# Larger q and k tiles in fewer buffers: 14, 12, 12 and 12 chunks with three buffers in place of five tiles of ten with four

## The chip, the core and the metric

The kernel runs on one core of a Trainium2 chip. The core has a matmul engine (PE, whose weight loads are listed apart as PEld), three engines for elementwise work (DVE, ACT and POOL), a queue engine (SP), and 16 DMA engines which all queues share. Each engine works through its own instructions in order; semaphores tie the engines together. The metric is the device time of one execution in microseconds. A DMA that changes the type of its data, here float32 in HBM to bfloat16 on the chip, is issued from POOL in this kernel.

## What is computed

Inputs are q, k and v of shape 4 x 6400 x 256 and the weights of a mixture of eight small adapters. For each of the four batches a 256 x 256 attention matrix is formed over the 6400 rows, applied to v, and every output row then gets the sum of its two best adapters:

```python
qn = q / (np.linalg.norm(q, axis=1, keepdims=True) + 1e-06)
kn = k / (np.linalg.norm(k, axis=1, keepdims=True) + 1e-06)
s = kn.transpose(0, 2, 1) @ qn / tau
a = softmax(s)                      # over the last axis
x = v @ a                           # 25600 rows of 256
logits = x @ w_gate                 # 8 experts, the best two kept
w = softmax over the two
out = x + sum over the two of w * ((x @ A[e]) @ B[e])
```

## The kernel before

A batch has 6400 rows, which are cut into 50 chunks of 128 rows. A chunk of q, k or v is 128 partitions by 256 elements. q and k of one chunk take 0.262 MB in HBM, v of one chunk 0.131 MB. All inputs together are 78.6 MB, the output is 26.2 MB.

**Two kinds of work.** The first is the Gram stage of a batch: for each chunk `gram` (L211) adds k transposed times q into the PSUM tile `acc` (two matmuls, L217), `square` (L199) squares two chunks of q and k, and `norm` (L222) adds up the squares by matmuls (L228 for batch 0, L234 for the others). When all 50 chunks are in, seven short functions `chain0` to `chain6` turn `acc` and the norms into the attention matrix `a_bf` and into `wa_sb`, the attention matrix times the gate and adapter weights. The second kind is the row stage: for each pair of chunks of v, `transposes` (L366) turns the rows over, `logits` and `gating` choose the experts for a group of five pairs, `z_gz` (L472, L476) multiplies by the adapters and weighs them by the gates into the tile `gz`, `gz_t` (L496 to L502) turns that over into `gzT`, `y_mm` (L488) multiplies v by the attention matrix, and `delta` (L508, L512) adds the adapters' part and copies the result to the staging tile `ys`.

**The order.** The whole order is written out by hand. Batch 0's Gram stage runs alone, at the beginning. After it come 100 slots, one for each pair of v's chunks, 25 to a batch, in one loop on all engines. In the loop the Gram stages of batches 1, 2 and 3 are spread over slots 0 to 20, 24 to 45 and 49 to 67, some two or three chunks to a slot (`todo`). A slot s transposes pair s; z, gz and y of a pair come several slots later, once its group's gates are ready. Chunk c of batch 1 falls in slot c*21//50, so that chunks 10 and 11 are in slot 4, chunk 14 in slot 5, chunk 26 in slot 10.

**Loads.** q and k of a batch come in five tiles of ten chunks (`PC = 10`), each filled by two DMAs (L148 for q, L149 for k). The first four chunks of batch 0 come on SP in float32 instead, and batch 0's last tile comes in parts of 6 and 4. v comes in tiles of 18, 16 and 16 chunks (L151), which for batch 0 are loaded in two parts each (10 and 8, 8 and 8, 8 and 8). There are four buffers for tiles of q and k and three for v. All these loads are in one list, sorted by the slot in which each is first needed. `qk_need` gives that slot for a tile of q and k; for v it is the number of the pair plus one. The sort keeps the order of the list where slots are equal, and q and k were put in first. `load_more` (L129) issues from the head of the list and stops at a tile whose buffer is still to be read by work not yet written out, so POOL issues loads in exactly this order. On POOL the issue waits for the release of the buffer, and everything behind it waits along.

Read in this order, the list before begins: batch 0's q and k; batch 1's q and k tile 0; the first part of v's first tile; q and k tile 1; the second part of v's first tile (v chunks 10 to 17); q and k tile 2; the first part of v's second tile (v chunks 18 to 25); q and k tile 3; and so on.

**Stores.** The output leaves from nine `ys` tiles of ten chunks. ACT issues the stores (L529). Up to seven finished groups are held back while loads are still to come (`DEFER`); from slot 67 on the number held back falls. The last ten pairs go out in smaller pieces on SP (L516).

**Working buffers.** `gz` and `gzT` rotate through three buffers each (`work`), and `ae`, the exponentiated attention matrix of a batch, through two (`bat`).

Of the kernel before, what the change touches and what calls it, by code (L numbers as in the profile page):

```python
# [9 lines left out]
BF16 = mybir.dt.bfloat16  # L10
# [6 lines left out]
def kernel(  # L17
# [17 lines left out]
    B, N, C = q.shape  # L35
    P = 128
    NC = N // P
    CC = C // P
# [3 lines left out]
    assert ER == P and CC == 2 and N % P == 0  # L42
    inv_tau = 1.0 / float(tau)

    PC = 10
    NPAIR = NC // 2
    NPT = B * NPAIR
    GRP = 5
    QKB, VB, YB = 4, 3, 9
    VP = [18, 16, 16]  # L50
    FIRST = 4
    DEFER = 7

# [9 lines left out]
    qk_pool = ctx.enter_context(tc.tile_pool(name="qkp", bufs=QKB))  # L63
    v_pool = ctx.enter_context(tc.tile_pool(name="vp", bufs=VB))
# [3 lines left out]
    bat = ctx.enter_context(tc.tile_pool(name="bat", bufs=2))  # L68
    one = ctx.enter_context(tc.tile_pool(name="one", bufs=1))
    gwork = ctx.enter_context(tc.tile_pool(name="gwork", bufs=3))  # L70
    work = ctx.enter_context(tc.tile_pool(name="work", bufs=3))
    ps_acc = ctx.enter_context(tc.tile_pool(name="psacc", bufs=1, space=bass.MemoryType.PSUM))
    ps_nrm = ctx.enter_context(tc.tile_pool(name="psnrm", bufs=1, space=bass.MemoryType.PSUM))
    ps_t = ctx.enter_context(tc.tile_pool(name="pst", bufs=2, space=bass.MemoryType.PSUM))
# [6 lines left out]

    todo = {}
    qk_need = {}
    for b, (first, last) in GRAM.items():
        n = last - first + 1
        for c in range(NC):
            s = first + c * n // NC
            todo.setdefault(s, []).append((b, c))
            qk_need.setdefault((b, c // PC), s)


    loads = []

    for s in range(NC // PC):
        o = FIRST if s == 0 else 0
        loads.append((-10 + s, "qk", 0, s, o, [6, 4] if s == NC // PC - 1 else [PC - o]))
        for b in range(1, B):
            loads.append((qk_need[b, s], "qk", b, s, 0, [PC]))
    for b in range(B):
        for s, n in enumerate(VP):  # L100
            at = NPAIR * b + sum(VP[:s]) // 2 + 1
            if b == 0:

                loads.append((at, "v", b, s, 0, [n - 8]))
                loads.append((at + (n - 8) // 2, "v", b, s, n - 8, [8]))
            else:
                loads.append((at, "v", b, s, 0,
                              [8, 4, 4] if b == B - 1 and s == len(VP) - 1 else [n]))
    loads.sort(key=lambda x: x[0])
    tiles = {"qk": {}, "v": {}}  # L110
    left = {"qk": [], "v": []}
    bufs = {"qk": QKB, "v": VB}
    where = {}
    at_load = [0]

    def piece(kind, c):

        if kind == "qk":
            return divmod(c, PC)
        s = 0  # L120
        while c >= VP[s]:
            c -= VP[s]
            s += 1
        return s, c

    def used(kind, b, c, n):
        left[kind][where[kind, b, piece(kind, c)[0]]] -= n

    def load_more(limit=1000):  # L129

        while limit and at_load[0] < len(loads):
            _, kind, b, s, o, parts = loads[at_load[0]]
            if (kind, b, s) not in where:
                n = len(left[kind])
                if n >= bufs[kind] and left[kind][n - bufs[kind]]:
                    return
                where[kind, b, s] = n
                left[kind].append(PC if kind == "qk" else VP[s])
                if kind == "qk":
                    t = qk_pool.tile([P, 2, PC, C], BF16, tag="qk", name="qk")  # L140
                else:
                    t = v_pool.tile([P, max(VP), C], BF16, tag="v", name="vt")
                tiles[kind][b, s] = t
            t = tiles[kind][b, s]
            c0 = s * PC if kind == "qk" else sum(VP[:s])
            for m in parts:
                if kind == "qk":
                    nc.gpsimd.dma_start(t[:, 0, o:o + m, :], q_v[b, :, c0 + o:c0 + o + m, :])  # L148
                    nc.gpsimd.dma_start(t[:, 1, o:o + m, :], k_v[b, :, c0 + o:c0 + o + m, :])  # L149
                else:  # L150
                    nc.gpsimd.dma_start(t[:, o:o + m, :], v_v[b, :, c0 + o:c0 + o + m, :])  # L151
                o += m
            at_load[0] += 1
            limit -= 1
# [11 lines left out]
    nc.sync.dma_start(bst, moe_B.rearrange("e r d -> (e r) d"))  # L166
    nc.sync.dma_start(ast, moe_A.rearrange("e (p cc) r -> p e (cc r)", p=P))
    load_more(3)
    ones_bf = const.tile([P, P], BF16)
    nc.vector.memset(ones_bf, 1.0)  # L170
# [4 lines left out]
    for c in range(0, FIRST, 2):  # L175
        t = tiles["qk"][0, 0]
        nc.vector.tensor_copy(t[:, 0, c:c + 2, :], stage[:, 0, c:c + 2, :])
        nc.scalar.copy(t[:, 1, c:c + 2, :], stage[:, 1, c:c + 2, :])
    load_more(1)
    ident = const.tile([P, P], BF16)  # L180
    make_identity(nc, ident)
    ident_f = const.tile([P, P], FP32)
    make_identity(nc, ident_f)
    load_more(3)

    wg_sb = const.tile([P, CC, E], BF16)
# [11 lines left out]

    def square(b, c, eng):  # L199

        s, o = divmod(c, PC)
        t = tiles["qk"][b, s]
        sq = sq_pool.tile([P, 2, 2, C], BF16, tag="sq", name="sq")
        sqs[b, c] = sq
        src = t[:, :, o:o + 2, :]
        if eng == "act":
            nc.scalar.activation(sq, src, ACT.Square)  # L207
        else:
            nc.vector.tensor_tensor(out=sq, in0=src, in1=src, op=OP.mult)  # L209

    def gram(b, c):  # L211
        if c == 0:
            acc[b] = ps_acc.tile([P, CC, C], FP32, tag="acc", name="acc")
        s, o = divmod(c, PC)
        t = tiles["qk"][b, s]
        for ic in range(CC):
            nc.tensor.matmul(  # L217
                acc[b][:, ic, :], t[:, 1, o, ic * P:(ic + 1) * P], t[:, 0, o, :],
                start=(c == 0 and ic == 0), stop=(c == NC - 1), skip_group_check=True)
        used("qk", b, c, 1)  # L220
# [60 lines left out]

    def chain3(b):
        d = st[b]
        ae = bat.tile([P, CC, C], BF16, name="ae")
        se = bat.tile([P, CC], FP32, name="se")
        for ic in range(CC):
            nc.scalar.activation(ae[:, ic, :], d["s"][:, ic, :], ACT.Exp, bias=neg_inv_tau[:, 0:1],
                                 scale=inv_tau, accum_out=se[:, ic:ic + 1])
        d["ae"], d["se"] = ae, se
# [37 lines left out]
    def chain6(b):  # L327
        d = st[b]
        a_bf = bat.tile([P, CC, C], BF16, name="a_bf")
        for ic in range(CC):  # L330
# [3 lines left out]


    CHAIN = [(chain0, 0.0), (chain1, 0.9), (chain2, 0.75), (chain3, 0.0), (chain4, 0.55),
             (chain5, 0.65), (chain6, 0.5)]

# [14 lines left out]
    def transposes(g, eng):  # L353

        b, p = divmod(g, NPAIR)
        gr = groups[g]
        if "vT" not in gr:
            gr["vT"] = vt_pool.tile([P, CC, 2 * GRP, P], BF16, tag="vT", name="vT")
        s, o = piece("v", 2 * p)
        vt = tiles["v"][b, s]  # L360
        full = ps_t.tile([P, 512], FP32, tag="pt", name="vT_ps")
        pt = full[:, 0:256].bitcast(BF16).rearrange("p (c t) -> p c t", c=CC)
        i = 0
        for sc in range(2):
            for ic in range(CC):
                nc.tensor.matmul(pt[:, ic, sc * P:(sc + 1) * P],  # L366
                                 vt[:, o + sc, ic * P:(ic + 1) * P], ident,
                                 is_transpose=True, start=(i == 0), stop=(i == 3))
                i += 1
        used("v", b, 2 * p, 2)  # L370
        w = 2 * (g - gr["f"])
        dst = gr["vT"][:, :, w:w + 2, :]
        src = pt.rearrange("p c (s t) -> p c s t", s=2)
        if eng == "act":
            nc.scalar.copy(dst, src)  # L375
        else:
            nc.vector.tensor_copy(dst, src)  # L377
        gr["full"] = full
        pr[g] = {"vT": dst, "w": w}
# [152 lines left out]
    for c in range(0, NC, 2):  # L532
        square(0, c, "act" if (c // 2) % 2 else "dve")
        gram(0, c)
        gram(0, c + 1)
        load_more()
        if c >= 4:
            norm(0, c - 4)
            norm(0, c - 3)
# [7 lines left out]
    def gram_part(items):  # L547
        for b, c in items:
            gram(b, c)
            if c >= 2:  # L550
                norm(b, c - 2)
            if c == NC - 1:
                norm(b, c - 1)
                norm(b, c)
# [18 lines left out]
    while nz < NPT or zq is not None or dq is not None:  # L573
# [7 lines left out]
        for b, c in items:  # L581
            if c % 2 == 0:
                square(b, c, "act")
        if f in (chain0, chain1, chain2, chain3):
            f(fb)
# [70 lines left out]
```

## Time and profile before

| | |
|---|---|
| median of three runs | 255.92 us (255.84 to 256.08) |
| the profiled execution | 255.87 us |
| its span, first to last instruction | 254.1 us |
| PE busy, share of the span | 220.4 us, 87% |
| ACT busy | 176.1 us, 69% |
| DVE busy | 152.7 us, 60% |
| POOL busy | 33.0 us, 13% |
| HBM read and written | 78.91 MB and 26.21 MB, 414 GB/s over the span |
| POOL's queue of loads | 8496 packets, 74.8% of the 16 DMA engines' time |
| ACT's queue of stores | 2592 packets, 22.4% |

Busy time of PE contains pipelined matmuls, so a busy PE is not one at its peak. GB/s in the slices and windows counts bytes as they land on the chip; a load is read from HBM at twice that, as it turns float32 into bfloat16. A DMA share can be above 1, since packets of one DMA engine overlap. "Time to landing" of an issue runs from the issue on the queue to the last byte's semaphore, with all that lies ahead of it in the DMA engines.

### The profile page before, as it was taken

Reading aid. Unit: us, or ns where it says so; the run is one execution under the profiler, and the core shown is the slowest. Engines: PE = TensorE matmul, PEld = TensorE weight load, DVE = VectorE, ACT = ScalarE, POOL = GpSimd, SP = SyncE. Lnnn points to the kernel's source line nnn. Section 1 sums busy time; section 2 is a strip of 40 time slices with the busy share of each in tenths; the row PEclk is TensorE's granted clock in tenths of the full one; section 3 lists DMA queues with packets and bytes.
Section 4 is the critical chain, followed back from the end, with each engine's and each line's share of the span. In section 5 each row is a group of like instructions: output and inputs, shape, how many; then the busy total and the mean of one; then the engine's idle time right before and its main releaser. Section 6 shows DMA issues by size and latency. Waiting matters only on the chain.

```text
span 254.1 us, 7393 instructions
## 1 busy us (share of the span) xinstructions
PE 220.4 (87%) x3106; PEld 190.2 (75%) x3106; DVE 152.7 (60%) x577; ACT 176.1 (69%) x290; POOL 33.0 (13%) x67
## 2 busy tenths in 40 slices
PE   0787793985999999999999989999999899999950
PEld 0444461775899978989999778989997799998940
DVE  1322235453567678685776876767587876778720
ACT  3434344776488698887878778888867777887860
POOL 8131221112112100110110202000000200000000
PEclk9999998696899999999999999999999999999997
DMA  7999999999999999999999999999999999999995
GB/s 213 223 217 215 212 216 214 213 216 216 210 214 215 223 207 215 218 212 214 215 220 211 214 270 259 236 296 281 255 291 292 389 326 362 414 420 426 423 412 220
DMA packets 13745, 66.80 MB, mean 263 GB/s; under 512 B 2576, under 2 KB 2704, under 8 KB 10384
## 3 DMA queue, kind: packets, MB, share of 16 engines
q0 software_dynamic: 8496, 38.80, 74.8%
q10 hardware_dynamic: 2592, 23.59, 22.4%
q1 hardware_dynamic: 2624, 3.94, 4.7%
q8 instruction: 24, 0.39, 0.6%
q14 instruction: 9, 0.07, 0.1%
HBM read 78.91 MB, written 26.21 MB: 414 GB/s over the span
## 4 chain that ended last, share of the span: by engine, by line
PE 58%; DMA 25%; DVE 7%; ACT 3%; issue 2%; POOL 1%; DVEq 0%; POOLq 0%; ACTq 0%
DMA qk<-in_k_dram 20%; PE y_ps L488 15%; PE acc L217 11%; PE zg L472 7%; PE y_ps L508 7%; PE vT_ps L366 6%; DMA out_dram<-ys 5%; PE zg L496 4%; PE nrm L234 3%; PE vT_ps L387 3%; ACT sq L207 2%; DVE gz L476 2%; ACT ys L512 1%; DVE lm L422 1%; DVE e L418 1%
## 5 line engine op out<-in xcount | busy, mean ns | idle before, releaser
L207 ACT ACTIVATE sq<-qk 128x1024 bf16<-128x1024 bf16 x87 | 89.6, 1054 | 22.1 <-DMA qk<-in_k_dram 16.8
L217 PE MATMUL acc<-qk 128*128 128x256 bf16 x400 | 74.7, 287 | 15.3 <-DMA qk<-in_k_dram 8.8
L512 ACT COPY ys<-y_ps 128x512 f32<-128x512 f32 x100 | 58.8, 588 | 22.9 <-PE y_ps L508 19.7
L488 PE MATMUL y_ps<-a_bf,vT 128*128 128x256 bf16 x400 | 60.3, 273 | 0.3 <-ACT ys L512 0.3
L217 PEld LDWEIGHTS <-qk 128*128 128x128 bf16 x400 | 34.4, 102 | 25.4 <-DMA qk<-in_k_dram 11.8
L476 DVE TENSOR_TENSOR gz<-zg,gate 128x256 bf16<-128x256 f32 x100 | 41.7, 418 | 14.7 <-PE zg L472 13.4
L377 DVE COPY vT<-vT_ps 128x512 bf16<-128x512 bf16 x63 | 26.7, 424 | 28.2 <-PE vT_ps L366 27.6
L234 PEld LDWEIGHTS <-sq 128*128 128x128 bf16 x600 | 36.3, 98 | 7.2 <-ACT sq L207 3.1
L366 PE MATMUL vT_ps<-ident,vt 128*128 128x128 bf16 x400 | 39.5, 223 | 0.9 <-DMA vt<-in_v_dram 0.7
L472 PE MATMUL zg<-wa_sb,vT 128*128 128x128 bf16 x400 | 38.7, 220 | 1.2 <-DVE gzT L502 1.0
L508 PE MATMUL y_ps<-ball_sb,gzT 128*128 128x256 bf16 x200 | 38.2, 273 | 0.0
L234 PE MATMUL nrm<-ones_bf,sq 128*128 128x1 bf16 x600 | 35.9, 165 | 1.2 <-ACT sq L207 1.2
L488 PEld LDWEIGHTS <-vT 128*128 128x128 bf16 x400 | 33.6, 97 | 3.2 <-issue 0.4
L366 PEld LDWEIGHTS <-vt 128*128 128x128 bf16 x400 | 30.2, 99 | 3.4 <-DMA vt<-in_v_dram 0.8
L496 PE MATMUL zg<-ident,gz 128*128 128x128 bf16 x200 | 27.9, 222 | 1.1 <-DVE gz L476 0.6
L375 ACT COPY vT<-vT_ps 128x512 bf16<-128x512 bf16 x37 | 21.7, 587 | 10.3 <-PE vT_ps L366 8.9
L472 PEld LDWEIGHTS <-vT 128*128 128x128 bf16 x400 | 26.1, 97 | 3.4 <-issue 2.2
L502 DVE COPY gzT<-zg 128x256 bf16<-128x256 bf16 x90 | 25.3, 281 | 0.0
L148 POOL DMA_DIRECT2D qk<-in_q_dram x21 | 11.4, 545 | 91.1 <-ACT sq L207 23.6
L209 DVE TENSOR_TENSOR sq<-qk 128x1024 bf16<-128x1024 bf16 x13 | 9.0, 693 | 22.3 <-DMA qk<-in_k_dram 15.4
L496 PEld LDWEIGHTS <-gz 128*128 128x128 bf16 x200 | 15.3, 99 | 2.9 <-DVE gz L476 2.5
L151 POOL DMA_DIRECT2D vt<-in_v_dram x17 | 9.0, 534 | 64.4 <-PE y_ps L508 45.5
(61 smaller groups left out, 183.6 us busy)
## 6 DMA issues: line engine op xcount, KB each, us to landing
out_dram<-ys ACTq DMA_DIRECT2D x18, 1280.0 KB, 13.1
qk<-in_q_dram POOLq DMA_DIRECT2D x18, 640.0 KB, 20.9
qk<-in_k_dram POOLq DMA_DIRECT2D x18, 640.0 KB, 23.1
vt<-in_v_dram POOLq DMA_DIRECT2D x5, 1024.0 KB, 26.9
vt<-in_v_dram POOLq DMA_DIRECT2D x3, 1152.0 KB, 25.3
vt<-in_v_dram POOLq DMA_DIRECT2D x6, 512.0 KB, 22.1
out_dram<-ys SPq DMA_DIRECT2D x3, 512.0 KB, 8.7
out_dram<-ys SPq DMA_DIRECT2D x4, 256.0 KB, 7.6
```

The source lines that it names most:

```text
L207: nc.scalar.activation(sq, src, ACT.Square)
L217: nc.tensor.matmul(acc[b][:, ic, :], t[:, 1, o, ic * P:(ic + 1) * P], t[:, 0, o, :], start=(c == 0 and ic == 0), stop=(c == NC - 1), skip_ ...
L234: nc.tensor.matmul(nrm[b][:, j:j + 1], sq[:, w, c % 2, ic * P:(ic + 1) * P], ones_bf[:, 0:1], start=(c == 0 and j == 0), stop=(c == NC - 1 ...
L366: nc.tensor.matmul(pt[:, ic, sc * P:(sc + 1) * P], vt[:, o + sc, ic * P:(ic + 1) * P], ident, is_transpose=True, start=(i == 0), stop=(i = ...
L377: nc.vector.tensor_copy(dst, src)
L472: nc.tensor.matmul(z[:, sc, :], r["vT"][:, ic, sc, :], st[b]["wa"][:, ic, E:E + ER], start=(sc == 0 and ic == 0), stop=(sc == 1 and ic == ...
L476: nc.vector.tensor_tensor(out=gz.rearrange("p c (e r) -> p c e r", e=E), in0=z.rearrange("p c (e r) -> p c e r", e=E), in1=gr["gate"][:, r ...
L488: nc.tensor.matmul(y[:, sc, :], r["vT"][:, ic, sc, :], st[b]["a"][:, ic, :], start=(sc == 0 and ic == 0), stop=False, skip_group_check=True)
L496: nc.tensor.matmul(gt[:, sc, :], r["gz"][:, sc, :], ident, is_transpose=True, start=(sc == 0), stop=(sc == 1))
L502: nc.vector.tensor_copy(gzT, gt)
L508: nc.tensor.matmul(r["y"][:, sc, :], r["gzT"][:, sc, :], ball_sb, start=False, stop=(sc == 1), skip_group_check=True)
L512: nc.scalar.copy(gr["ys"][:, r["w"]:r["w"] + 2, :], r["y"])
```

## The change

Tiles of q and k have 14, 12, 12 and 12 chunks in place of five times 10, and three buffers in place of four. Batch 0's last tile is loaded in parts of 8 and 4. The helper `piece`, which used to look up v's uneven tiles, now serves q and k too; the lists of sizes stand together in `PARTS`. The tile in memory always has room for 14 chunks, so three of them take 43,008 bytes of a partition where four of ten chunks took 40,960. `work` goes from three buffers to two, and `ae` from two to one, which frees 2,048 bytes between them. Nothing else differs: the order of the matmuls, squares and copies is the same.

```diff
-    PC = 10
-    QKB, VB, YB = 4, 3, 9
-    VP = [18, 16, 16]
+    QKB, VB, YB = 3, 3, 9
+    PARTS = {"qk": [14, 12, 12, 12], "v": [18, 16, 16]}
...
-    work = ctx.enter_context(tc.tile_pool(name="work", bufs=3))
+    work = ctx.enter_context(tc.tile_pool(name="work", bufs=2))
...
+    def piece(kind, c):
+        s = 0
+        while c >= PARTS[kind][s]:
+            c -= PARTS[kind][s]
+            s += 1
+        return s, c
+
...
-            qk_need.setdefault((b, c // PC), s)
+            qk_need.setdefault((b, piece("qk", c)[0]), s)
...
-    for s in range(NC // PC):
+    for s, n in enumerate(PARTS["qk"]):
         o = FIRST if s == 0 else 0
-        loads.append((-10 + s, "qk", 0, s, o, [6, 4] if s == NC // PC - 1 else [PC - o]))
+        last = s == len(PARTS["qk"]) - 1
+        loads.append((-10 + s, "qk", 0, s, o, [n - 4, 4] if last else [n - o]))
         for b in range(1, B):
-            loads.append((qk_need[b, s], "qk", b, s, 0, [PC]))
+            loads.append((qk_need[b, s], "qk", b, s, 0, [n]))
...
-                    t = qk_pool.tile([P, 2, PC, C], BF16, tag="qk", name="qk")
+                    t = qk_pool.tile([P, 2, max(PARTS[kind]), C], BF16, tag="qk", name="qk")
...
-            c0 = s * PC if kind == "qk" else sum(VP[:s])
+            c0 = sum(PARTS[kind][:s])
...
-        s, o = divmod(c, PC)
+        s, o = piece("qk", c)
...
-        ae = bat.tile([P, CC, C], BF16, name="ae")
+        ae = one.tile([P, CC, C], BF16, name="ae")
```

More of the change, by code (lines that the diff above doesn't have):

```diff
@@ L88 @@
             todo.setdefault(s, []).append((b, c))
-            qk_need.setdefault((b, c // PC), s)
+            qk_need.setdefault((b, piece("qk", c)[0]), s)
     loads = []
-    for s in range(NC // PC):
+    for s, n in enumerate(PARTS["qk"]):
         o = FIRST if s == 0 else 0
-        loads.append((-10 + s, "qk", 0, s, o, [6, 4] if s == NC // PC - 1 else [PC - o]))
+        last = s == len(PARTS["qk"]) - 1
+        loads.append((-10 + s, "qk", 0, s, o, [n - 4, 4] if last else [n - o]))
         for b in range(1, B):
-            loads.append((qk_need[b, s], "qk", b, s, 0, [PC]))
+            loads.append((qk_need[b, s], "qk", b, s, 0, [n]))
     for b in range(B):
-        for s, n in enumerate(VP):
-            at = NPAIR * b + sum(VP[:s]) // 2 + 1
+        for s, n in enumerate(PARTS["v"]):
+            at = NPAIR * b + sum(PARTS["v"][:s]) // 2 + 1
             if b == 0:
@@ L107 @@
                 loads.append((at, "v", b, s, 0,
-                              [8, 4, 4] if b == B - 1 and s == len(VP) - 1 else [n]))
+                              [8, 4, 4] if b == B - 1 and s == len(PARTS["v"]) - 1 else [n]))
     loads.sort(key=lambda x: x[0])
@@ L114 @@
     at_load = [0]
[L116 to L124, printed above, removed]
     def used(kind, b, c, n):
@@ L137, in load_more @@
                 where[kind, b, s] = n
-                left[kind].append(PC if kind == "qk" else VP[s])
+                left[kind].append(PARTS[kind][s])
                 if kind == "qk":
-                    t = qk_pool.tile([P, 2, PC, C], BF16, tag="qk", name="qk")
+                    t = qk_pool.tile([P, 2, max(PARTS[kind]), C], BF16, tag="qk", name="qk")
                 else:
-                    t = v_pool.tile([P, max(VP), C], BF16, tag="v", name="vt")
+                    t = v_pool.tile([P, max(PARTS[kind]), C], BF16, tag="v", name="vt")
                 tiles[kind][b, s] = t
             t = tiles[kind][b, s]
-            c0 = s * PC if kind == "qk" else sum(VP[:s])
+            c0 = sum(PARTS[kind][:s])
             for m in parts:
@@ L213, in gram @@
             acc[b] = ps_acc.tile([P, CC, C], FP32, tag="acc", name="acc")
-        s, o = divmod(c, PC)
+        s, o = piece("qk", c)
         t = tiles["qk"][b, s]
```

## The prediction

> **What bounds the kernel now.** I read first the slices of the page, then a table of 5 us windows. Its columns are stretch, length, busy time (x instructions) of PE, PEld, DVE, ACT and POOL, granted PE clock, share of the DMA engines' time, GB/s.
>
> ```profile
> DMA  7999999999999999999999999999999999999995
> ...
> 15.00:20.00 5.00, 3.93 (x29) 2.75 (x29) 1.39 (x2) 3.14 (x3) 1.98 (x4) 1.00 1.10 217
> 55.00:60.00 5.00, 2.35 (x43) 2.02 (x42) 3.03 (x14) 1.47 (x4) 0.53 (x1) 0.92 1.05 213
> 60.00:65.00 5.00, 5.00 (x53) 4.32 (x52) 2.10 (x6) 3.72 (x4) 1.06 (x2) 0.50 1.07 218
> 75.00:80.00 5.00, 5.00 (x95) 4.72 (x91) 3.43 (x15) 4.40 (x8) 0.87 (x2) 1.00 1.06 213
> 245.00:250.00 5.00, 0.47 (x5) 0.18 (x2) 0.00 (x0) 1.02 (x2) 0.00 (x0) 1.00 0.96 390
> ```
>
> Two limits lie close together. The DMA engines are full from 5 us to 249 us, so the bytes alone nearly fill the span. PE waits for loads up to about 62 us (3.93 and 2.35 busy of 5), and from then on is busy 4.5 to 5.0 of 5 until the last work at 246 us. So 62 to 246 us is a nearly rigid train of slots: what is late at 62 us is late at 246 us. The PE timeline shows the waits where the train starts:
>
> ```profile
> 53.64 0.40 PE L366 MATMUL vT_ps<-ident,vt 128*128 128x128 bf16 x4 [0.71 <-DMA vt<-in_v_dram]
> 56.73 0.38 PE L472 MATMUL zg<-wa_sb,vT 128*128 128x128 bf16 x4
> 59.77 0.61 PE L217 MATMUL acc<-qk 128*128 128x256 bf16 x2 [2.65 <-DMA qk<-in_k_dram]
> ...
> 62.45 0.59 PE L366 MATMUL vT_ps<-ident,vt 128*128 128x128 bf16 x4
> ```
>
> 53.64 is slot 5, which transposes chunks 10 and 11 of v; 62.45 is slot 9, chunks 18 and 19. Both pieces are in the views of single issues of line 151: issue time, then time to landing.
>
> ```profile
> L151 POOL DMA_DIRECT2D vt<-in_v_dram x1: 530/530/530, 32.6 to 32.6; - x1
> ...
> DMA to landing us min/median/max: 21.0/21.0/21.0
> ...
> L151 POOL DMA_DIRECT2D vt<-in_v_dram x1: 527/527/527, 39.1 to 39.1; - x1
> ...
> DMA to landing us min/median/max: 23.0/23.0/23.0
> ```
>
> They land at 53.6 and 62.1 us. The tail and one late wait come from the same view of the last store, and from the list of waits:
>
> ```profile
> L516 SPq DMA_DIRECT2D out_dram<-ys x1: 462/462/462, 246.1 to 246.1; - x1
> ...
> DMA to landing us min/median/max: 6.9/6.9/6.9
> ...
> ACT ys L512 <- DMA out_dram<-ys: 1.7, 1, 1.7
> ```
>
> **The change, part by part.** *Landing order.* POOL issues the loads in one sorted list, and the DMA engines work it off in that order. A chunk of q and k is 0.262 MB in HBM, a chunk of v half that. In the list before, 20 chunks of batch 1's q and k (tiles 0 and 1) stand ahead of the second piece of v's first tile, and 30 ahead of v's chunk 18. In the new list these are 14 + 12 = 26, and 14 + 12 + 12 = 38: the third tile's first use and this v piece both fall on slot 10, and the sort keeps q and k first. The read rate comes from landings: batch 0's last k (12.06 MB read) at 16.41 + 19.37 = 35.8 us, v's chunk 18 (23.33 MB) at 62.1, so 26.3 us for 11.27 MB, 2.33 us per MB. Six more chunks are 1.57 MB or 3.7 us, eight are 2.10 MB or 4.9 us. The two v pieces land at 57.3 and 67.0 us. Nothing covers this: slot 5 is already waiting at 53.64, and slot 9 cannot transpose before 67.0, 4.55 us after 62.45. Queued behind that wait is all of PE; DVE's vT copy and ACT's squares and copies follow it.
>
> *The clock.* After the 2.65 us wait PE ran at half clock (0.50 in 60:65; normal slots return at 66). Slots 9 to 12 took 62.45 to 70.16, 7.7 us with 3.5 of it at half clock, against 4 slots in 8.04 us later (68.31 to 76.35), 6.0 for three. PE will now stand some 3.5 us ahead of slot 5 and 1.5 to 4 us ahead of slot 9. If the clock stays full, three slots take 6.0 and the train is 4.55 - 1.7 = 2.9 us late; with the 6.2 us of half clock that the 59.8 wait brought (1.7/3.5 us lost per us) it is 4.55 + 1.3 = 5.9. The wait ahead of slot 9 follows a stretch that will be slow already, so I lean to the upper half: 5.0. The Trainium skill ("TensorE: Matmul & The Clock Gate", Part 1: The HAM clock gate) speaks against the change here: an idle window of about 3.4 us halves the clock, a busy one of that length restores it. By this rule alone 3.4 us would be slow after 67.0, as many as before, so 4.5 us late and an end of about 257.0.
>
> *Phase 0.* The last piece but one is 8 chunks for 6. It lands 1.05 MB (2.5 us) before 35.8, so at 33.3, and PE needs 4 pairs of 0.87 us (0.87 is the step from 16.09 to 16.97): ready for the last piece at 36.8, 1.0 us late. Slot 0 goes from 46.5 to 47.5, and its first v piece lands at 47.4 too, 4 chunks later than 45.0. Both end in the wait of slot 5: nothing more.
>
> *Fewer, larger transfers.* q and k go from 21 to 17 DMAs each. Eight issues of 0.53 us leave POOL, which is 13% busy: nothing. On the DMA engines the saving is not shown: at least 0; at most one mean packet (74.8% of 16 x 254.1 us over 8496 packets, 0.36 us) for each of 8, 2.9 us. I take 0.3, near the bottom, since stretches of 10-chunk q/k transfers and of 16 and 18-chunk v ones run alike at 213 to 216 GB/s. The Trainium skill ("DMA: Bandwidth & Descriptors", Anatomy of one DMA) gives each such DMA a fixed 2.0 us beside its bytes; eight fewer in series would be 16 us, an end near 240. The landings agree with bytes alone, since seven others are in flight.
>
> *Three buffers of q/k.* A load now waits on the tile three back. The tightest is batch 3's first: released at slot 35 (118.3 us, and some 6 later now), while the load ahead of it lands at 128.8 as before (102.30 + 26.5). The margin falls from 17.6 us (issued at 111.2) to about 4.7. The shortest landing of a POOL load is 6.3 us (the first, 0.79 MB, 1.8 us of it bytes): 4.5 us of start. It just holds: cost 0, at most 1.8 us at each of four such waits. v's loads stand behind it on POOL.
>
> *Two buffers of gz and gzT, one of ae.* DVE's gz write waits for the transposes of two slots ago, its gzT copy for the delta matmuls two before; PE is in order and has done both ahead of the matmuls that DVE waits for anyway. Cost 0. Uncovered, each of 100 slots could pay a PE group of 0.28 us. ae of the batch before was last read 20 slots earlier: 0.
>
> *The sum.* The train is 5.0 late. At 194.6 ACT waited 1.7 us for a store to free a ys buffer; stores will find the DMA engines less loaded, and this wait goes. PE lost 0.5 of 5 us in 191:196, so 0.6 comes back: 4.4. What of it shows? The last store took 6.9 us to land, behind others, where the first load (0.52 MB, empty queues) took 3.6: up to 3.3 us are hidden by the queue. On the other side the DMA share is already 0.98 in 196:199, so idle DMA time there may be added in full: 0 hidden. I take 2.5, nearer the last store's own row, as it is the one that ends the run. 4.4 - 2.5 - 0.3 = 1.6. Profiled run 255.87 us (span 254.1, 1.8 around it; median of three 255.92): **257.5 us**. Its own range: 2.9 late, 3.3 hidden, 0.3 saved, 255.5; 5.9 late, none hidden, 260.9, of which I keep 259.5.
>
> **The rivals.** *Not slower: the tail hides it all.* The DMA engines are the sole bound; bytes are equal; the lateness stays below the 3.3 us of queue. For it: the full DMA row. Against: 4.4 is above 3.3. It decides if the clock stays full at slot 9: 2.9 - 0.6 = 2.3. Time 255.87 - 0.3 = 255.6; with more saved per transfer, up to 2.9, 253.0. *Starved queue.* The 4.7 us margin is too short and loads stop at four releases, while stores are still held back. For it: half of the margin gone. Against: 15 us and more in hand today. Two to four stops of 1.8 us take the place of the hidden part: 259.5. *The two-buffer wait bites*: 100 slots of 0.28 us, 284; the program order speaks against it.
>
> **How the numbers follow.** Forecast 0.70, hidden tail 0.18, starved queue 0.10, buffers 0.02. What a measurement can tell from no change is 0.2%, 0.5 us. Of the forecast, 0.04 falls below 256.4 (same) and none lower; the hidden tail splits 0.13 faster, 0.05 same. Faster 0.13, same 0.09, slower 0.78. The range takes the forecast's own and reaches into the hidden tail: 255.3 to 259.8.
>
> **What would show it.** Right: slot 5's transposes near 57.3 and slot 9's near 67.0, each ended by a v load; half clock reaching 70 us or beyond; the last ys copy near 250; the wait of 1.7 us on ys gone; a shorter landing of the last store. Wrong: slot 9 before 64, a later v piece without a later end, or DMA slices below 9 between 110 and 170 us (then the queue starves).

## The result, and the profile after

| | before | after |
|---|---|---|
| median of five runs | 256.02 us (255.84 to 256.08) | 259.38 us (258.52 to 259.94) |
| ratio, 95% interval | | 1.013 (1.0105 to 1.0154) |
| the profiled execution | 255.87 us | 259.80 us |
| its span | 254.1 us | 258.0 us |
| HBM rate over the span | 414 GB/s | 407 GB/s |
| packets on POOL's queue, share of the DMA engines' time | 8496, 74.8% | 7344, 73.8% |
| last `ys` copy ends | 246.09 us | 251.14 us |

The change costs 3.4 us by the medians, 3.9 us between the two profiled executions. The forecast was 257.5 us: right in direction, and less than half of the loss.

The PE timeline of after, at the two waits for v (start, length, engine, line, operation, and in brackets the idle time before it with what ended it):

```profile
57.23 0.40 PE L365 MATMUL vT_ps<-ident,vt 128*128 128x128 bf16 x4 [2.30 <-DMA vt<-in_v_dram]
...
67.06 0.61 PE L365 MATMUL vT_ps<-ident,vt 128*128 128x128 bf16 x4 [3.44 <-DMA vt<-in_v_dram]
...
70.56 0.63 PE L365 MATMUL vT_ps<-ident,vt 128*128 128x128 bf16 x4
```

Slot 5 starts at 57.23 and slot 9 at 67.06, both ended by the landing of a v piece; the forecast had 57.3 and 67.0. Slot 9 now sits 4.61 us behind its old 62.45. It runs at half clock (0.61 us for four transposes where 0.40 is normal), and slot 11 starts at 73.62 us, 5.31 us late. From there the train is rigid: 5.31 at slot 62, 5.50 at slot 71, 4.95 at slot 74, 5.05 at the last `ys` copy.

Both pieces again in the views of single issues:

```profile
L150 POOL DMA_DIRECT2D vt<-in_v_dram x1: 550/550/550, 35.4 to 35.4; - x1
...
DMA to landing us min/median/max: 21.7/21.7/21.7
...
L150 POOL DMA_DIRECT2D vt<-in_v_dram x1: 558/558/558, 40.7 to 40.7; - x1
...
DMA to landing us min/median/max: 26.4/26.4/26.4
```

They are issued 2.8 and 1.6 us later than before, and the second has 3.4 us more ahead of it in the DMA engines (26.4 against 23.0).

The row of DMA slices and the windows of after, with the columns of the windows before (the last three are PE clock, DMA share, GB/s):

```profile
DMA  7999999999999999999999999999999999999994
...
55.00:60.00 5.00, 2.77 (x53) 2.46 (x54) 2.14 (x9) 1.65 (x3) 2.12 (x4) 0.89 1.06 216
60.00:65.00 5.00, 3.63 (x48) 3.18 (x46) 2.86 (x11) 4.23 (x6) 0.00 (x0) 0.77 1.03 212
65.00:70.00 5.00, 2.94 (x30) 2.50 (x31) 1.04 (x3) 0.74 (x1) 0.00 (x0) 0.57 1.06 215
...
153.00:154.00 1.00, 1.00 (x33) 0.97 (x31) 0.67 (x2) 1.00 (x6) 0.00 (x0) 1.00 1.15 160
154.00:155.00 1.00, 0.80 (x13) 0.52 (x10) 0.68 (x4) 1.00 (x3) 0.00 (x0) 1.00 0.97 129
...
190.00:195.00 5.00, 5.00 (x80) 4.57 (x79) 4.35 (x19) 3.74 (x9) 0.53 (x1) 1.00 0.87 240
...
207.00:208.00 1.00, 0.96 (x12) 0.91 (x13) 0.97 (x6) 0.36 (x2) 0.00 (x0) 1.00 0.82 182
...
250.00:255.00 5.00, 0.52 (x5) 0.21 (x3) 0.00 (x0) 1.07 (x2) 0.00 (x0) 0.85 0.93 366
```

The same stretches of before:

```profile
153.00:154.00 1.00, 0.81 (x18) 0.78 (x18) 0.97 (x7) 1.00 (x2) 0.56 (x2) 1.00 0.99 317
154.00:155.00 1.00, 1.00 (x20) 0.87 (x17) 0.40 (x2) 1.00 (x3) 1.00 (x2) 1.00 1.05 329
...
190.00:195.00 5.00, 4.67 (x70) 4.07 (x68) 3.86 (x15) 3.10 (x7) 0.00 (x0) 1.00 1.01 261
...
207.00:208.00 1.00, 1.00 (x21) 0.96 (x18) 0.67 (x3) 0.57 (x2) 0.00 (x0) 1.00 0.98 297
```

PE does 3.63 and 2.94 us of work in 60:65 and 65:70, where it did 5.00 in 60:65 before. Further down three stretches stand out that the kernel before does not have. At 153 to 155 us the DMA engines move 160 and 129 GB/s, where loads alone run at 212 to 216 (the rows from 55 to 70 us). Over 190:195 their share is 0.87 (1.01 before). At 207 they fall to 182 GB/s. In all three PE is busy for 0.80 of the time or more, so its column shows nothing of this; at 153 us the DMA share, 1.15, does not show it either.

The view of the last store of after (issue, then time to landing), and ACT's waits for a free `ys` buffer from 100 us on (total, times, longest):

```profile
L515 SPq DMA_DIRECT2D out_dram<-ys x1: 1066/1066/1066, 251.2 to 251.2; - x1
...
DMA to landing us min/median/max: 5.8/5.8/5.8
```

```profile
ACT ys L511 <- DMA out_dram<-ys: 2.4, 2, 1.6
```

The last store is issued 5.05 us later than before and lands 5.8 us after its issue instead of 6.9. Only 1.1 us of the lateness is hidden. The late wait for a `ys` buffer, 1.7 us at slot 72 before, has become two earlier ones of 1.6 and 0.8 us, which end at 178.8 and 189.5 us.

**Counting bytes instead of waits.** The packets of a trace also tell how many bytes have moved by a given time (a packet under way counts by the part of its time that has passed). A load on POOL's queue counts with the bytes read from HBM, twice those that land. In the kernel before this sum goes from 24.43 MB at 60 us to 100.96 MB at 240, so 0.425 MB per us. What another kernel has moved less by some moment, divided by 0.425, is the time that its DMA engines have lost so far. For after:

```
by (us)             100     145     165     190     195     210     230   | span
lost (us)          -0.24   0.03    0.92    0.90    2.29    3.36    3.43  | +3.94
```

The engines lose 0.9 us between 145 and 165, 1.4 between 190 and 195 and 1.1 between 195 and 210. These are the three thin stretches of the windows, and together they are 3.4 us of the 3.94. Elsewhere little is lost: 0.3 between 100 and 145, and 0.5 after 230. The late slots at 57 and 67 us cost the DMA engines nothing at that time. This count tells when time is lost, not why: all versions move the same bytes, so what is short at 230 us has to be made up behind it.

### The profile page after: what moved, and what is told of

The parts are those of the page before. It is cut to its first block, busy times and chain, and to the rows that moved or that the text cites. A ratio compares the mean times of both kernels' runs of the same rounds, so it can differ in the third digit from the quotient of the medians.

```text
span 258.0 us, 7398 instructions
## 1 busy us (share of the span) xinstructions
PE 223.1 (86%) x3106; PEld 192.3 (75%) x3106; DVE 152.7 (59%) x577; ACT 176.4 (68%) x290; POOL 28.6 (11%) x59
## 3 DMA queue, kind: packets, MB, share of 16 engines
q0 software_dynamic: 7344, 38.80, 73.8%
q1 hardware_dynamic: 2624, 3.94, 4.7%
## 4 chain that ended last, share of the span: by engine, by line
PE 58%; DMA 24%; DVE 7%; ACT 4%; issue 2%; POOL 1%; DVEq 0%; ACTq 0%; POOLq 0%
PE y_ps L487 14%; PE acc L216 10%; DMA vt<-in_v_dram 10%; DMA qk<-in_k_dram 9%; PE zg L471 7%; PE y_ps L507 7%; PE vT_ps L365 6%; DMA out_dram<-ys 5%; PE zg L495 4%; PE vT_ps L386 3%; PE nrm L233 3%; ACT sq L206 3%; PE nrm L227 2%; DVE gz L475 2%; ACT ys L511 1%
## 5 line engine op out<-in xcount | busy, mean ns | idle before, releaser
L216 PE MATMUL acc<-qk 128*128 128x256 bf16 x400 | 76.7, 294 | 12.7 <-DMA qk<-in_k_dram 6.5
L216 PEld LDWEIGHTS <-qk 128*128 128x128 bf16 x400 | 35.3, 104 | 23.0 <-DMA qk<-in_k_dram 7.9
L233 PEld LDWEIGHTS <-sq 128*128 128x128 bf16 x600 | 37.0, 99 | 7.5 <-ACT sq L206 2.8
L147 POOL DMA_DIRECT2D qk<-in_q_dram x17 | 9.3, 546 | 132.8 <-ACT ys L511 49.4
L227 PE MATMUL nrm<-sq,ones_bf 128*128 128x512 bf16 x50 | 16.9, 430 | 0.0
```

Source lines behind the costliest of these rows:

```text
L216: nc.tensor.matmul(acc[b][:, ic, :], t[:, 1, o, ic * P:(ic + 1) * P], t[:, 0, o, :], start=(c == 0 and ic == 0), stop=(c == NC - 1), skip_ ...
L233: nc.tensor.matmul(nrm[b][:, j:j + 1], sq[:, w, c % 2, ic * P:(ic + 1) * P], ones_bf[:, 0:1], start=(c == 0 and j == 0), stop=(c == NC - 1 ...
```

## The experiments

The theory after the result: one tie in the sorted list puts a tile of twelve q and k chunks ahead of v's chunk 18; the train starts 5 us late; some of this is hidden at the end, less than forecast because the DMA engines run thin later on. Rivals: the three buffers by themselves; the small working buffers; the larger transfers.

**e1. The working buffers alone**, in the kernel before.

```diff
-    work = ctx.enter_context(tc.tile_pool(name="work", bufs=3))
+    work = ctx.enter_context(tc.tile_pool(name="work", bufs=2))
...
-        ae = bat.tile([P, CC, C], BF16, name="ae")
+        ae = one.tile([P, CC, C], BF16, name="ae")
```

> Tiles of ten and four buffers as before; only gz, gzT in two buffers and ae in one. Landing-order theory: these waits are covered by PE's own order, so 255.9 us, within 0.3 of before. Rival (the small buffers cost part of the 3.4 us): 256.5 or more, and gz or gzT writes on DVE would show idle time ended by PE in steps of 0.2 to 0.3 us.

256.13 us against 256.07, ratio 1.0001 (0.9993 to 1.001). They cost nothing.

**e2. The changed kernel with q and k of batches 1 to 3 loaded in smaller parts**, cut at chunks 10, 20, 30 and 40, each part due by its own first chunk. The tiles and the three buffers stay.

```diff
...
-            loads.append((qk_need[b, s], "qk", b, s, 0, [n]))
+            c0 = sum(PARTS["qk"][:s])
+            cuts = [c0] + [x for x in (10, 20, 30, 40) if c0 < x < c0 + n] + [c0 + n]
+            for lo, hi in zip(cuts, cuts[1:]):
+                loads.append((chunk_need[b, lo], "qk", b, s, lo - c0, [hi - lo]))
```

> The changed kernel's tiles and its three buffers, but the loads of batches 1 to 3 are cut at chunks 10, 20, 30 and 40 and each part is put in the list by its own first use, so that bytes land in the order they had before. Landing-order theory: the v pieces of slots 5 and 9 land near 53.6 and 62.1 us again, slot 9 starts near 62.5 and not at 67, and the time is 255.6 to 256.5 us. Rival (three buffers starve the load queue, or the tiles' size itself costs): still 258.5 us or more.

257.02 us, ratio 1.0047 (1.0031 to 1.0062): 2.4 us of the 3.4 come back, not all, and the time is above the 256.5 that the theory allowed. The profiled execution is the slowest of its six, 258.08 us. In it slot 9 is at 62.18 us, near the 62.45 of the kernel before, and the train is 0.65 us late up to slot 40. So the landing order is what delayed it. Then something new takes 2.5 us. ACT's timeline (an engine name with a q is its instruction queue):

```profile
146.56 4.09 ACTq L531 DMA_DIRECT2D out_dram<-ys  x1
...
150.70 2.00 ACT L209 ACTIVATE sq<-qk 128x1024 bf16<-128x1024 bf16 x2 [1.25 <-issue]
```

The issue of the first store takes 4.09 us, where ACT's others take 0.34 to 0.63; ACT stands still for 1.25 us, PE waits 1.7 us for its squares, and 3.4 us at half clock follow. Why this one issue is slow is open.

**e3. The changed kernel with v first where slots are equal.** One word in the sort, nothing else.

```diff
-    loads.sort(key=lambda x: x[0])
+    loads.sort(key=lambda x: (x[0], x[1] == "qk"))
```

> The changed kernel with one rule added: where a v tile and a q/k tile are first needed in the same slot, v is loaded first. Landing-order theory: v's chunk 18 lands near 59.7 us and q/k's chunk 26 near 67.0; slot 9 starts before 65, and slot 10 waits in its place, about one slot of work later, so lateness falls from 5 us to between 1 and 3, and the time to 256.0 to 257.5 us. Rival (starved queue): unchanged, 258.5 us or more.

255.93 us against 256.07, ratio 0.9992 (0.9983 to 1.0), better than expected. PE timeline:

```profile
57.03 0.40 PE L365 MATMUL vT_ps<-ident,vt 128*128 128x128 bf16 x4 [3.09 <-DMA vt<-in_v_dram]
...
63.46 0.38 PE L365 MATMUL vT_ps<-ident,vt 128*128 128x128 bf16 x4
```

Slot 5 still waits until 57.0, so the larger first tiles still cost there; slot 9 starts at 63.46 without a wait, and the last `ys` copy is 0.67 us late. The larger tiles, the three buffers and the small working buffers are all still in place. So the loss hangs on the order at equal slots. This word turns round two ties, not one: at slot 10, and at slot 35, where a v tile of batch 1 meets a q and k tile of batch 2. The second had no part in the lateness: in the changed kernel that v tile lands at 115.2 us, and slot 34, which needs it, starts at 121.4.

**e4. Three buffers of ten chunks**, in the kernel before.

```diff
-    QKB, VB, YB = 4, 3, 9
+    QKB, VB, YB = 3, 3, 9
```

> The kernel before with three buffers of ten chunks of q and k in place of four; order and sizes as before. Landing-order theory: 255.7 to 256.5 us, since a load still has 3 to 8 us in hand at its latest release. Rival (three buffers starve the load queue): 257.5 us or more, with windows of the DMA share below 0.95 between 110 and 170 us.

258.06 us, ratio 1.0069 (1.0046 to 1.0091): a miss. Windows of 2 us, then the PE timeline:

```profile
152.00:154.00 2.00, 1.81 (x29) 1.46 (x27) 1.96 (x10) 1.68 (x3) 0.23 (x1) 1.00 0.79 294
154.00:156.00 2.00, 2.00 (x35) 1.81 (x33) 1.21 (x5) 2.00 (x4) 1.35 (x3) 1.00 0.80 136
```

```profile
171.21 0.40 PE L366 MATMUL vT_ps<-ident,vt 128*128 128x128 bf16 x4 [0.99 <-DMA vt<-in_v_dram]
```

The train is 0.3 us late up to slot 50, then the DMA share falls to 0.8 at 152 to 156 us and a v tile lands late. Three buffers of ten (30 chunks) starve the engines by themselves; three of 14 and 12 in e3 do not.

**e5. The changed kernel, six groups of stores held back** instead of seven.

```diff
-    DEFER = 7
+    DEFER = 6
```

> The changed kernel, but six finished groups of output are held back in place of seven, so that one store of 1.31 MB (3 us of the DMA engines) leaves some ten slots earlier. Theory A (the lateness of 5 us shows in full but for 1.1 us because the DMA engines run dry near 190 to 206 us while stores are held back): PE's train stays some 5 us late, the DMA windows there stay at 0.99 or more, the last store lands in 3.6 to 5.0 us in place of 5.8, and the time falls by 0.8 to 2 us, to 257.4 to 258.6. Theory B (the end is the train's end plus a fixed landing): 259.4, within 0.5.

256.64 us, ratio 1.003 (1.0019 to 1.0042): 2.7 us faster than the changed kernel, more than expected. The train is nearly as late as there: 4.53 us at slot 11 (5.31 there) and 4.35 at the end (5.05). A window of 2 us where the changed kernel is thin, first of the changed kernel and then of this one, and the view of the last store:

```profile
192.00:194.00 2.00, 2.00 (x38) 1.90 (x36) 1.70 (x8) 1.76 (x6) 0.01 (x1) 1.00 0.91 158
192.00:194.00 2.00, 2.00 (x37) 1.90 (x36) 1.62 (x7) 1.23 (x4) 0.00 (x0) 1.00 1.02 298
```

```profile
DMA to landing us min/median/max: 3.1/3.1/3.1
```

The engines stay full here, and the last store lands in 3.1 us in place of the 6.9 of the kernel before: 3.8 of 4.35 us are hidden. A train nearly as late costs 0.6 us if the engines are fed, and 3.4 if not.

**e6. The kernel before, batch 1's q and k tiles 2 to 4 loaded in parts of 4 and 6 chunks, v first**, to start the train earlier than ever.

```diff
...
-            loads.append((qk_need[b, s], "qk", b, s, 0, [PC]))
+            cut = 4 if b == 1 and s >= 2 else PC
+            loads.append((chunk_need[b, s * PC], "qk", b, s, 0, [cut]))
+            if cut < PC:
+                loads.append((chunk_need[b, s * PC + cut], "qk", b, s, cut, [PC - cut]))
...
-    loads.sort(key=lambda x: x[0])
+    loads.sort(key=lambda x: (x[0], x[1] == "qk"))
```

> The kernel before with batch 1's q/k tiles 2, 3 and 4 loaded in parts of 4 and 6 chunks, each due at its own first use, and v first where slots are equal. Buffers and tiles as before. Landing-order theory: slot 8 starts near 57.3 without a wait, slot 9 near 59.5, slot 12 near 67 in place of 70.2; the train runs 2 to 3 us ahead of before, and half of that or less shows, as the bytes bound stands at about 251: 254.3 to 255.6 us. Rival (the bytes alone end the kernel, the train matters only when late): 255.7 to 256.3.

256.39 us, ratio 1.0016 (1.0007 to 1.0025): a miss. The train is 2.6 us ahead at slot 8 and 1.0 ahead at slot 40. Then the first store issue on ACT is slow, as in e2, the train is 1.9 us late at slot 52, and the end is 1.36 late. ACT's timeline:

```profile
144.88 4.17 ACTq L532 DMA_DIRECT2D out_dram<-ys  x1
```

**e7. The kernel before, v's chunks 18 to 25 behind one more q and k tile.** Tiles of ten, four buffers: the suspected cause alone.

```diff
-    loads.sort(key=lambda x: x[0])
+    loads.sort(key=lambda x: 12 if x[:5] == (10, "v", 0, 1, 0) else x[0])
```

> The kernel before with one load moved: the first part of v's second tile (chunk 18 on) goes behind q/k tile 3 of batch 1 in place of ahead of it. Tiles, buffers and sizes as before. Landing-order theory: this part lands near 68.3 us, slot 9 starts there, 5.9 us late, half clock adds up to 1.3, and the train carries it to the end: lateness 5.5 to 7.2 us at the last store, time 259.5 to 262 us. Rival (four buffers of ten hide it; the loss belongs to three large buffers): 256 to 257.5.

260.82 us, ratio 1.0191 (1.0173 to 1.0208). PE timeline and windows of 2 us:

```profile
68.38 0.61 PE L366 MATMUL vT_ps<-ident,vt 128*128 128x128 bf16 x4 [6.52 <-DMA vt<-in_v_dram]
```

```profile
188.00:190.00 2.00, 2.00 (x33) 1.88 (x31) 1.05 (x3) 2.00 (x4) 0.00 (x0) 1.00 0.52 203
...
192.00:194.00 2.00, 2.00 (x35) 1.88 (x33) 1.81 (x10) 1.12 (x4) 0.53 (x1) 1.00 0.28 106
```

Slot 9 starts at 68.38, 5.93 us late (68.3 was worked out from the bytes ahead), the end is 6.68 late, and the engines run nearly dry between 186 and 195 us. With four buffers nothing is lost at 153 us. A late v piece makes the loss without any of the change's other parts.

**e8. The changed kernel, v first, batch 1's q and k tiles 1 to 3 loaded in halves of six.**

```diff
...
-            loads.append((qk_need[b, s], "qk", b, s, 0, [n]))
+            c0 = sum(PARTS["qk"][:s])
+            cut = 6 if b == 1 and s >= 1 else n
+            loads.append((chunk_need[b, c0], "qk", b, s, 0, [cut]))
+            if cut < n:
+                loads.append((chunk_need[b, c0 + cut], "qk", b, s, cut, [n - cut]))
...
-    loads.sort(key=lambda x: x[0])
+    loads.sort(key=lambda x: (x[0], x[1] == "qk"))
```

> The changed kernel's tiles and buffers, v first where slots are equal, and batch 1's tiles 1, 2 and 3 loaded in halves of six chunks, each due at its own first use. Landing-order theory: v's chunks 10 and 18 land near 53.7 and 59.8, slot 9 starts near 60.5, and the train runs 1.5 to 3 us ahead of the kernel before; the time is 254.5 to 255.7 us. Rival (bytes alone): 255.7 to 256.3.

256.77 us, ratio 1.0027 (1.0016 to 1.0038): a miss. The train is 2.4 to 4.2 us ahead from slot 8 to slot 23 and waits at slot 25:

```profile
95.99 0.40 PE L369 MATMUL vT_ps<-ident,vt 128*128 128x128 bf16 x4 [3.14 <-DMA vt<-in_v_dram]
```

Batch 1's first v tile stands behind batch 2's 14-chunk tile. It is the same order of landings, met one batch later, because the train came early.

**e9. v first, and six groups held back.** e3 and e5 in one.

> The changed kernel with v ahead of q and k where slots tie (lateness 0.67 us at the end when this was done alone, 255.93 us) and six groups of stores held back in place of seven (2.7 us less alone, on a train 4.5 us late). Theory A, held-back stores cost only where the train is late (what sending sooner gains is tail, and the tail cannot go below the train's own end): the end of the work stays at the e3 place, about 246.8 us, the last store's landing is at least 3.1 us after it, so the gain is at most 255.93 - (250.6 + 1.8) of 3.5 us, but the bytes then need more rate than the engines gave; 254.5 to 255.9 us. Theory B, sending sooner moves loads back instead and only helps a train that is late anyway: 255.9 to 257.5 us, with a new wait for a v or a q/k load on PE after slot 13.

258.89 us against 256.22, ratio 1.0096 (1.0082 to 1.011). Theory B, and worse than it said. PE timeline:

```profile
183.34 0.61 PE L216 MATMUL acc<-qk 128*128 128x256 bf16 x2 [4.25 <-DMA qk<-in_k_dram]
```

The train is 0.5 us late until slot 52. The stores that leave sooner stand ahead of loads which the early train needs: the k load issued at 157 us takes 25.9 us to land, against 19.8 in e3. Batch 3's Gram stage waits 4.25 us, 6.8 us of half clock overlap this wait and what follows it, and the end is 7.4 us late.

**e10. The kernel before, six groups held back**: the control for e5.

> The kernel before with six groups of stores held back in place of seven; nothing else. It is the control for the 2.7 us that sending sooner took off the changed kernel. Theory A, the engines ran dry at 190 to 206 us only because the train was late with three buffers: in the kernel before the DMA share is 1.00 or above from 180 to 210 us, so sending sooner has no dry time to fill and gives 255.4 to 256.6 us. Theory B, sending sooner is good by itself, whatever the train: 253.2 to 254.5 us, and then the 2.7 us says nothing about what the late train cost.

256.89 us, ratio 1.0021 (1.0012 to 1.003): above the ranges of both theories, nearer theory A's (255.4 to 256.6). PE timeline, and the last store's view:

```profile
173.38 0.40 PE L366 MATMUL vT_ps<-ident,vt 128*128 128x128 bf16 x4 [3.77 <-DMA vt<-in_v_dram]
```

```profile
DMA to landing us min/median/max: 3.5/3.5/3.5
```

Here too a load is late because stores went first: the v load issued at 141 us takes 32.3 us to land, against 26.9 in the kernel before, and the train ends 4.43 us late. Yet the time is only 0.7 us longer, since the engines lose little (1.0 us up to 230 us, in the table below) and the last store lands in 3.5 us. This is nearly the lateness of after, at a fifth of its price.

No version beat the kernel before; e3 equals it.

**All runs side by side.** Lateness of the last `ys` copy, time lost by the DMA engines at 230 us (counted in bytes, as above), and the growth of the span, all from the one profiled execution of each, against the profile before, in us:

```
                                        late at end   lost at 230   span
e3  v first                                 0.67          0.00      -0.3
e1  small working buffers                   0.38          0.27      +0.5
e5  changed, stores sooner                  4.35          0.72      +0.5
e6  before, batch 1 in parts                1.36          0.85      +0.5
e10 before, stores sooner                   4.43          1.02      +1.0
e8  halves, v first                         1.51          1.15      +0.9
e2  changed, loads cut                      2.78          2.04      +2.2
e4  before, three buffers                   1.81          2.46      +2.7
e9  v first, stores sooner                  7.38          2.71      +3.1
after                                       5.05          3.43      +3.9
e7  before, one v piece late                6.68          5.16      +5.6
```

The middle column follows the right one within 0.5 us in every row; being a count of the same bytes, it says in which stretch a version loses, and leaves the cause to the edits. The left column does not follow: 4.4 us late costs 0.5 or 1.0, 1.8 late costs 2.7.

## Why the prediction was right, and where it failed

**Landing order: right.** 57.3 and 67.0 forecast, 57.23 and 67.06 measured, from bytes ahead in the list at 2.33 us per MB. e3 and e7 show that this order is the cause: taken away, the loss goes; made by itself, a larger loss comes. The train was as rigid as forecast, 5.31 us late at slot 11 and at slot 62, although the rows of before go lower than the 4.5 busy of 5 that the prediction reads from them (4.32 in 145:150).

**Clock: right in kind, and the size partly by luck.** 5.0 us late forecast, with 2.9 and 5.9 as bounds; 5.31 measured at slot 11. The granted clock is 0.50 from 58.9 to 62.3 and from 65.8 to 72.6 us: 3.4 and 6.8 us. The Trainium skill ("TensorE: Matmul & The Clock Gate", Part 1: The HAM clock gate) gives a free-running window of about 3.4 us, and the stretches here are one and two of it. For this execution the sum by one window alone (4.5 us late) was too low. In e5, with the same order of loads and a wait of 3.42 us ahead of slot 9 where after has 3.44, there is one stretch only, from 68.0 to 71.4 us, and slot 11 is 4.53 us late, as that sum has it. So whether such a wait brings one stretch or two differs between executions, and 5.0 lay between. Nor did PE have to idle for 3.4 us without a break: the stretch at 58.9 us follows a wait of 2.30, and the one at 65.8 begins 2.1 us into the wait of 3.44.

**Phase 0: hidden, as forecast.** Slot 0 came 1.65 us late instead of 1.0, with a stretch of half clock at 28.2 to 31.6 us; the wait at slot 5 took it in.

**Fewer transfers: 0.3 forecast, nothing clear seen.** e3 keeps them and has 0.9983 to 1.0 of the time before, a gain of 0.4 us at most with everything else in it. The Trainium skill ("DMA: Bandwidth & Descriptors", Anatomy of one DMA) has about 2.0 us of fixed cost for each such DMA; of eight fewer in a full queue 0.4 us at most can be seen here.

**Small working buffers: right.** e1.

**The wait for `ys`: gone at its place, but paid elsewhere.** The train regains 0.55 us at slots 72 to 74, as forecast (0.6); two new waits ahead of it, 1.6 and 0.8 us, take back 0.2, and another 0.1 goes later. Net 0.26.

**The step that failed: what is hidden at the end.** The prediction put it so: "up to 3.3 us are hidden by the queue ... I take 2.5, nearer the last store's own row". Measured: 1.1. With 5.31 late, 0.26 regained, 1.1 hidden and nothing saved the sum is 3.95, and 259.80 - 255.87 is 3.93. Of the 2.3 us that the forecast was short for this execution, 1.4 is this term; 0.3 each are the lateness, the `ys` wait and the transfers. The prediction sized this term by one row, the landing of the last store, as if the DMA engines would go on as before under a late train. They did not: in after three thin stretches lose 3.4 us. The last store's landing of 6.9 us in the kernel before says that the DMA engines, not PE, end it. What a late train costs is then, as far as these runs go, the time in which the engines are not fed while it is late; the lateness itself is hidden up to the point where the last store meets an empty queue. In e5 and e10, where the engines are fed, 3.8 and 3.4 us are hidden, about the bound of 3.3 that the prediction took from the first load's landing. The prediction's own lower bound of this term (0 hidden) named the reason (idle DMA time at the end "may be added in full"), but looked for it in 196 to 199 us of the old profile and gave it little weight.

**The rival of the starved queue was half right**, and its 259.5 is nearest to the result, in part by luck: it counted two to four stops at the buffers. Its margins were sized well: the loads that wait for a third buffer were issued 3.8 to 4.8 us ahead of the previous landing at 111, 123, 145 and 161 us in after, against 4.7 forecast. One of the four had a loss behind it, the one at 145.6, with 0.9 us at 153 to 156 (that this wait caused it is argued from the times, not tried alone). In e5, with the same three buffers, the load is issued at 144.8 us and nothing is lost there: a first store had left at 141.8, and the landing ahead of the load came 8.2 us after its issue in place of 4.2. The sign that the prediction named for a starved queue, DMA slices below 9 between 110 and 170 us, did not appear, since the share hides this loss. The other 2.5 us are lost after 190 us, when stores are still held back and loads wait for a late train: a v load issued at 191.47, 5.5 us later than before, finds its queue empty and lands in 7.9 us. But the three buffers do not starve the engines alone; in e3 they are there and nothing is lost. The late train thins the queue, and e7 shows it does so with four buffers as well.

**The hidden tail** (255.6) was wrong for this change. e3 comes near it with 255.93, but with only 0.67 us of lateness to hide. **The two-buffer wait** is excluded by e1.

## What to carry to other kernels

When a kernel ends with a long last store, count bytes moved by a given time in the trace. In the eleven versions here the change of the end was the time that the DMA engines lost, within 0.5 us, and lateness of the compute engines counted only as far as it left them unfed. Making tiles larger changes the order in which a single sorted queue delivers; check each tie and each first use against what now stands ahead of it, in bytes. Stores held back to give loads the way are sized for one timing of the train. With the late train one group fewer gained 2.7 us; with the train on time it cost 0.7 us in the kernel before and 3.0 in e3.

## What the runs showed of the hardware

A thin DMA queue does not have to show in its busy share: at 153 to 154 us of after the share is 1.15 while the rate is 160 GB/s, and the slices of after read 9 in the DMA row there. The share counts how long packets are under way, not what they move.

Two kernels with more and smaller loads (e2, e6) had a first store issue on ACT of 4.09 and 4.17 us, at 146.6 and 144.9 us, where all other store issues there took below 0.7. e8 has smaller loads too and shows no such issue (its first takes 0.37). The cause is open.

The half-clock stretches before 75 us are 3.41 us or a multiple of it in every profile, but lie at different times from kernel to kernel: 42.1 to 48.9 and 59.2 to 66.0 before; 28.2 to 31.6, 45.3 to 52.1, 58.9 to 62.3 and 65.8 to 72.6 after. The five runs of after spread over 1.4 us where those of before spread over 0.24; that the phase of these stretches is the reason was not tried.
